# Block attention and gated MLP on one core: a first load on another queue, a transpose on another engine, and load issues at another place in the order

## Chip, cores and metric

One core of a Trainium2 chip runs the whole program. The metric is device time in microseconds of one execution; the lower, the better. The three executions shown of the kernel before took 164.96, 169.21 and 168.84 us, with a median of 168.84 us. The profiled execution is the one of 164.96 us.

## The reference, cut to what matters

There are 4 batches of 8 heads, 768 rows and 64 columns per head. A row of `q`, `k`, `v` blocks is 96 long, and there are 8 blocks.

```
P = sort_net                                  # (4, 8, 8, 8)
for _ in range(5):                            # Sinkhorn
    P = exp(P - max(P, -1));  P = P / sum(P, -1);  P = P / sum(P, -2)
k_sorted, v_sorted = P mixes the 8 blocks of k and of v
scores = q_block @ k_sorted_block.T / 8       # 96 x 96, block by block
x = softmax(scores) @ v_sorted_block          # -> (4, 768, 512)
h = relu(x @ w_in);  u, v = halves of h
v_s = w_spatial @ normalize(v) + b_spatial
out = (u * v_s) @ w_out                       # (4, 768, 512) float32
```

## The kernel before

**Inputs.** `load_heads` (L91) loads one batch of `q`, `k` or `v` as a tile of 128 partitions, 8 heads and 384 columns. The source is fp32 and the tile bf16; the DMA is issued by POOL and casts on the way. The tiles `q_in`, `k_in` and `v_in` have two buffers each, so batches 0 and 1 are loaded at the start. POOL's issues stand in this order: q and k of batch 0 (L101, L102), v of batch 0 (L128), `w_in` (L130), the bias (L131), `w_spatial` (L133), v, k and q of batch 1 (L134 to L136), `w_out` (L138). Among them POOL builds an identity and two selection masks (`ident_bf`, `a16`, `sel16`). SP carries the small load of `sort_net` (L88), the two-step turn of the mixed v through HBM (`vd`, `vb`, L263 and L264), and the results.

**The mixing matrix.** `sinkhorn` (L150) alternates one exponential on ACT (L152) with six small operations on DVE, five times, and leaves `p_bf` of 32 partitions (batch and head) by 8 by 8. `spread_t` (L177) turns it with eight matmuls and a DVE copy into `pt`; `spread` (L189) then spreads it over 128 partitions with one matmul and a DVE copy into `prep_sb`. `make_pdiag` (L199) multiplies that by a mask and gives `pdiag`, one 128 x 128 matrix per head, by which the matmuls of `ktr`, `vtr` and `vmix` mix blocks. Batch 0 is spread before the schedule. Its other three batches come by steps P and R in the schedule, with their `make_pdiag` on POOL.

**The order.** Inside `manual_schedule` the order of PE, DVE, ACT and POOL is written out by hand in `SCHEDULE` (L482). A step such as `k30A1` is a unit (`k`), its index (3), the batch (0), the engine that empties PSUM (A for ACT, D for DVE) and one of four PSUM buffers (1). Units of attention: `k` and `q` transpose, `v` (and `t`, `B` for batch 0) mixes v, `s` scores with an exponential on ACT, `a` attends and takes a logarithm on ACT, `d` divides. Units of the MLP: `V`, `N` (normalize), `U`, `S` (spatial matmul), `O` (output), `w` turns `w_spatial`. The MLP of one batch is interleaved with the attention of the next. Each engine takes its own instructions strictly in that order.

**The gates.** A unit S of the MLP (L437) adds the bias on DVE (`vs`, L454, two buffers) and multiplies by `u` on POOL (`gt`, L455); in the last batch DVE does both, in halves of 384 columns. Four `gt` feed the O units, in the order of their index. Before the first S of batches 0 and 1, POOL copies one element of each half of the next batch's `vb` (`gate`, L537). That makes it wait until both halves have landed. It then issues the loads of v, q and k for the batch after (L540 to L542), and only then its first `gt`.

**Elsewhere.** `warm` (L167) issues matmuls whose result nobody reads.

Of the kernel before, what the change touches and what calls it, by code (L numbers as in the profile page):

```python
# [8 lines left out]
FP32 = mybir.dt.float32  # L9
BF16 = mybir.dt.bfloat16  # L10
# [19 lines left out]
def kernel(  # L30
# [12 lines left out]
    nc = tc.nc  # L43
# [18 lines left out]
    pd_pool = ctx.enter_context(tc.tile_pool(name="pd", bufs=B))  # L62
    ld = ctx.enter_context(tc.tile_pool(name="ld", bufs=2))
    att = ctx.enter_context(tc.tile_pool(name="att", bufs=2))
    qk_pool = ctx.enter_context(tc.tile_pool(name="qk", bufs=7))
    ex_pool = ctx.enter_context(tc.tile_pool(name="ex", bufs=7))
# [3 lines left out]
    vs_pool = ctx.enter_context(tc.tile_pool(name="vs", bufs=2))  # L70
# [20 lines left out]
    def load_heads(x, b, name):  # L91
# [9 lines left out]
    q_in[0] = load_heads(q, 0, "q_in")  # L101
    k_in[0] = load_heads(k, 0, "k_in")  # L102
# [10 lines left out]
    sel16 = const.tile([8, 128], BF16)  # L113
    nc.gpsimd.memset(sel16, 0.0)
    nc.gpsimd.affine_select(
        out=sel16.rearrange("p (j t) -> p j t", t=TB),
        in_=sel16.rearrange("p (j t) -> p j t", t=TB),
        pattern=[[1, NB], [0, TB]], compare_op=ALU.not_equal,
# [54 lines left out]


    pts = {}

    def spread_t(b, nb, ps):  # L177
# [19 lines left out]
    pdiag = [pd_pool.tile([128, H, NB, TB], BF16, name="pdiag") for _ in range(B)]  # L197

    def make_pdiag(b, eng, h0, n):  # L199
        eng.tensor_mul(  # L200
            out=pdiag[b][:, h0:h0 + n],
            in0=_raw_ap(mask16, 0, [mask16.ap[0], [0, n], [TB, NB], [1, TB]]),
            in1=_raw_ap(prep_sb, b * NB * H + h0, [prep_sb.ap[0], [1, n], [H, NB], [0, TB]]),
        )
# [29 lines left out]
    class Attention:  # L234
# [147 lines left out]
    class Gmlp:  # L382
# [54 lines left out]
        def spatial(self, mc, eng, ps):  # L437
            t = ps_tile(ps)
            pairs = [(g, x) for g in range(G) for x in range(2)]
            if self.last:  # L440
                pairs = [(g, x) for x in range(2) for g in range(G)]
# [11 lines left out]
            for x in (slice(0, 1), slice(1, 2)) if self.last else (slice(0, 2),):  # L453
# [29 lines left out]
        k00A0 k30A1 k20D2 s00-3 k10D0 s70-1 s50-2 t30D3 t10A0 t00D1 s20-2 s60-3 B30D0 s10-1  # L483
        B10D2 s30-3 t20D0 a70-1 s40-2 B00D3 d70-- a20-0 B20D2 d20-- a00-3 a10-1 d00-- a40-2
        d10-- d40-- a30-0 a50-3 d30-- a60-1 P00-2 d50-- d60-- R00-0 V00-2 w50A3 w30A1 V10-0
        w40D2 v11A3 V20-1 v01A0 U00D3 v21A2 v31A1 U10A0 w20D2 w10D1 w00A3 k11D0 k21A2 q01D1
        k01A3 q11D0 k31D2 N00-- s31-1 U20A3 s11-0 s21-1 S00-2 s61-3 s41-0 U30A1 s51-2 s01-3
        S10-0 a01-1 d01-- a41-2 d41-- S20-3 a11-0 a51-1 d51-- d11-- S30-2 s71-3 a21-1 a61-0
        a31-2 d61-- d31-- O20A3 a71-0 d21-- O10A2 d71-- O00A3 V01-1 V21-2 v02A0 V11-3 v12A1
        U01A2 U11D0 N01-- v22A3 v32A1 U21A2 k12A0 q12D3 k02A1 q02A2 k22A0 k32A3 S01-1 s42-2  # L490
        s02-0 S11-3 s72-1 s52-2 S21-0 s32-3 s22-1 U31A2 a42-0 a02-3 d42-- d02-- s12-1 S31-2
        s62-0 a32-3 a72-1 d32-- a12-2 d72-- d12-- O21A0 a52-3 d52-- a22-1 a62-2 d22-- d62--
        O01D0 O11D3 V02-1 V22-2 v03A0 V12-3 v13A1 U02A2 U12D0 N02-- v23A3 v33A1 U22A2 k13A0
        q13D3 k03A1 q03A2 k23A0 k33A3 S02-1 s43-2 s03-0 S12-3 s73-1 s53-2 S22-0 s33-3 s23-1
# [82 lines left out]
```

The softmax here doesn't subtract the row's maximum and nothing guards it: scores larger than these inputs give would overflow.

## Time and profile before

| what | value |
| --- | --- |
| profiled execution, its own time | 164.96 us |
| its span (first to last instruction) | 163.2 us |
| three executions, median | 168.84 us (164.96 to 169.21) |
| PE busy | 147.4 us, 90% of the span |
| ACT, DVE, POOL busy | 109.9, 97.4, 42.8 us |
| landing of q, k, v of batch 0, from the span's start | 8.6, 12.4, 16.2 us |
| landing of v, k, q of batch 1 | 32.9, 36.8, 40.7 us |

The span is counted from the first recorded instruction to the last. The 1.76 us between the span and the execution's own time lie around it. A landing is an issue's start plus the time to landing that the profile gives for it. The chain of waits follows the work that ended last back from the end: at each step to what released it, or to the instruction before it on its engine. PE is busy 12.68 us of the 13 from 28 to 41 us, 49.74 of the 50 from 89 to 139 us, and 18.38 of the last 25.

### The profile page before, as it was taken

The numbers are of one execution on the slowest core, as the hardware profiler recorded it, in microseconds if no ns is written. First come the engines' busy times: TensorE is split into PE (matmuls) and PEld (weight loads), VectorE is DVE, ScalarE is ACT, GpSimd is POOL, SyncE is SP. The second block draws the span as 40 slices with busy tenths as digits, with TensorE's granted clock in tenths as the row PEclk, the third lists the DMA queues.
The fourth block names the chain that finished last, engine by engine and source line by source line (L and its number), as shares of the span: only waits on it lengthen the run. The fifth ranks groups of instructions, "written<-read, shape, count | busy, mean of one in ns | idle before, by whom it ended". The sixth has DMA issues, their size and how long they took to land.

```text
span 163.2 us, 3907 instructions
## 1 busy us (share of the span) xinstructions
PE 147.4 (90%) x1636; PEld 86.1 (53%) x1645; DVE 97.4 (60%) x203; ACT 109.9 (67%) x181; POOL 42.8 (26%) x46
## 2 busy tenths in 40 slices
PE   0969995999999999999995999999999999999770
PEld 0246872557756544457663544468556444565330
DVE  4667877468952652489222448785244478849951
ACT  3166999678787678689946892799778955550040
POOL 7941000890019740000069420000352400000000
PEclk9999999999999999999999999999999999999999
DMA  2999999999956999515429993525300036000055
GB/s 14 194 204 207 214 269 189 204 204 216 280 144 78 203 203 253 231 52 167 152 33 183 204 230 118 223 96 197 96 4 0 4 135 257 0 0 4 0 192 193
DMA packets 21554, 23.86 MB, mean 146 GB/s; under 512 B 736, under 2 KB 18144, under 8 KB 21408
## 3 DMA queue, kind: packets, MB, share of 16 engines
q0 software_dynamic: 13760, 12.58, 48.3%
q1 hardware_dynamic: 7776, 11.02, 18.8%
q8 instruction: 13, 0.21, 0.5%
q14 instruction: 5, 0.04, 0.1%
HBM read 27.14 MB, written 8.65 MB: 219 GB/s over the span
## 4 chain that ended last, share of the span: by engine, by line
PE 53%; DMA 24%; POOL 7%; DVE 6%; issue 6%; ACT 2%; DVEq 0%; POOLq 0%; SPq 0%
DMA q_in<-in_q_dram 19%; PE ps L443 13%; PE ps L465 10%; PE ps L393 9%; PE ps L428 8%; PE ps L352 4%; DVE vs L454 3%; PE ps L331 3%; PE ps L359 2%; DMA vb<-vd 2%; DVE gt L455 2%; PE ps L276 2%; POOL k_in L93 2%; DMA vd<-vm 1%; POOL v_in L93 1%
## 5 line engine op out<-in xcount | busy, mean ns | idle before, releaser
L443 PE MATMUL ps<-wspT,v_sb 128*128 128x384 bf16 x192 | 33.4, 327 | 0.0
L338 ACT ACTIVATE ex<-ps 96x768 bf16<-96x768 f32 x32 | 24.3, 806 | 7.0 <-PE ps L331 6.9
L454 DVE TENSOR_TENSOR vs<-ps,b_bc 128x768 f32<-128x768 f32 (+1 forms) x20 | 15.9, 795 | 21.6 <-PE ps L443 17.4
L375 DVE TENSOR_TENSOR xt<-ps,lns 128x384 bf16<-128x384 f32 x32 | 16.9, 554 | 19.7 <-ACT lns L371 19.7
L455 POOL TENSOR_TENSOR gt<-vs,u_sb 128x768 bf16<-128x768 f32 x12 | 19.6, 1653 | 31.5 <-ACT ex L338 29.7
L443 PEld LDWEIGHTS <-v_sb 128*128 128x128 bf16 x192 | 17.8, 98 | 11.8 <-issue 0.4
L465 PE MATMUL ps<-w_out_sb,gt 128*128 128x512 bf16 x90 | 21.9, 380 | 1.1 <-DVE gt L455 0.8
L428 PE MATMUL ps<-xt,w_in_sb 128*128 128x384 bf16 x128 | 22.6, 326 | 0.0
L393 PE MATMUL ps<-w_in_sb,xt 128*128 128x512 bf16 x94 | 22.1, 379 | 0.1
L407 DVE BATCH_NORM_STATS2 stats<-v_sb 128x6 f32<-128x512 bf16 x24 | 16.3, 678 | 8.5 <-ACT v_sb L227 8.4
L227 ACT ACTIVATE v_sb<-ps 128x1024 bf16<-128x1024 f32 (+1 forms) x15 | 12.5, 852 | 12.9 <-PE ps L393 12.9
L221 ACT COPY o_sb<-ps 128x256 f32<-128x256 f32 (+1 forms) x11 | 7.3, 663 | 13.8 <-DVE o_sb L223 12.1
L428 PEld LDWEIGHTS <-w_in_sb 128*128 128x128 bf16 x128 | 12.2, 98 | 8.1
L365 ACT ACTIVATE lns<-ps 128x384 f32<-128x384 f32 x32 | 14.4, 486 | 3.0 <-PE ps L359 3.0
L371 ACT ACTIVATE lns<-lns 128x384 f32<-128x384 f32 x32 | 15.7, 525 | 0.2
L465 PEld LDWEIGHTS <-gt 128*128 128x128 bf16 x96 | 8.6, 98 | 12.4 <-DVE gt L455 1.3
L393 PEld LDWEIGHTS <-xt 128*128 128x128 bf16 x96 | 9.2, 98 | 10.9 <-DVE xt L375 0.8
L352 PE MATMUL ps<-ex,vb 96*64 96x96 bf16 x256 | 11.3, 209 | 2.6 <-DVE vs L454 1.7
L352 PEld LDWEIGHTS <-vb 96*64 96x64 bf16 x256 | 8.6, 109 | 7.7 <-issue 6.4
L227 ACT ACTIVATE u_sb<-ps 128x768 bf16<-128x768 f32 x13 | 10.3, 808 | 1.7 <-PE ps L428 1.2
L221 ACT CAST kT<-ps 128x768 bf16<-128x768 f32 x13 | 10.0, 805 | 1.8 <-PE ps L288 1.8
L359 PE MATMUL ps<-ex,ones 96*64 96x384 bf16 x64 | 10.8, 326 | 0.0
(73 smaller groups left out, 174.5 us busy)
## 6 DMA issues: line engine op xcount, KB each, us to landing
out_dram<-o_sb SPq DMA_DIRECT2D x9, 512.0 KB, 2.8
q_in<-in_q_dram POOLq DMA_DIRECT2D x4, 768.0 KB, 10.3
k_in<-in_k_dram POOLq DMA_DIRECT2D x4, 768.0 KB, 13.6
v_in<-in_v_dram POOLq DMA_DIRECT2D x4, 768.0 KB, 9.7
vd<-vm SPq DMA_DIRECT2D x6, 384.0 KB, 4.0
vb<-vd SPq DMA_DIRECT2D x6, 384.0 KB, 3.7
out_dram<-o_sb SPq DMA_DIRECT2D x6, 256.0 KB, 2.1
wsp_nat<-in_moe_w_spatial_dram POOLq DMA_DIRECT2D x1, 1152.0 KB, 22.2
```

The lines of the kernel that those rows point to most:

```text
L221: nc.scalar.copy(out=out, in_=in_)
L227: nc.scalar.activation(out=out, in_=in_, func=AF.Relu)
L338: nc.scalar.activation(out=e.rearrange("p h i c -> p h (i c)"), in_=t[0:BLK, :, 0:NB // 2 * BLK], func=AF.Exp, scale=scale,)
L352: nc.tensor.matmul(t[hh * 64:hh * 64 + 64, 0, ii * BLK:(ii + 1) * BLK], lhsT=self.vb[:, i, h // (H // 2), h % (H // 2), :], rhs=self.e[n][ ...
L375: nc.vector.tensor_mul(out=self.xt[hp].rearrange("p (g i t) -> p i g t", g=G, i=NB)[:, i0:i0 + NB // 2], in0=t[:, 0, 0:HW].rearrange("p (i ...
L393: nc.tensor.matmul(t[:, x, :], lhsT=self.xt[kc][:, g * 128:(g + 1) * 128], rhs=w_in_sb[:, kc, DH:DFF], start=(kc == 0), stop=(kc == KC - 1),)
L407: nc.vector.bn_stats(out=stats, in_=v_sb[:, x, :])
L428: nc.tensor.matmul(t[:, x, 0:HW], lhsT=w_in_sb[:, kc, mc * 128:(mc + 1) * 128], rhs=self.xt[kc][:, x * HW:(x + 1) * HW], start=(kc == 0), ...
L443: nc.tensor.matmul(t[:, x, 0:HW], lhsT=self.v[g][:, mc * 128:(mc + 1) * 128], rhs=wspT[:, g, x * HW:(x + 1) * HW], start=(g == 0), stop=(g ...
L454: nc.vector.tensor_add(out=vs[:, x], in0=t[:, x, 0:HW], in1=b2[:, x])
L455: eng.tensor_mul(out=gt2[:, x], in0=vs[:, x], in1=u2[:, x])
L465: nc.tensor.matmul(t[:, x, :], lhsT=self.gt[mc][:, g * 128:(g + 1) * 128], rhs=w_out_sb[:, mc, :], start=(mc == 0), stop=(mc == FC - 1),)
```

## The change

The first q goes through SP's hardware queue as fp32 into a tile `q_first` and is cast by two copies on POOL and two on ACT. The ACT copies stand in the fourth round of Sinkhorn, and the transposes of q in the fifth. The tile `wsp_nat` takes over the buffer of `q_first`. The load of k stands behind the masks on POOL, and one mask is larger (32 x 512). `p_bf` is turned by two DVE transposes once for all batches; eight matmuls spread it. The first two heads of `pdiag` are made from PSUM. Batches 1 to 3 are spread at the schedule's start. In each attend of batch 0 three matmuls of 128 columns are added, whose result nobody reads. The gate and the loads behind it stand before the third S instead of the first. In the last batch only the last S stays on DVE in halves; the other three are whole, with `gt` on POOL. `ex` has eight buffers (seven before), `vs` three (two before). The schedule is written anew for batches 0 and 1; for 2 and 3 only PSUM buffers 0 and 2 change places.

```diff
--- before.py
+++ after.py
@@ -60,14 +60,15 @@
     const = ctx.enter_context(tc.tile_pool(name="const", bufs=1))
     pers = ctx.enter_context(tc.tile_pool(name="pers", bufs=1))
     pd_pool = ctx.enter_context(tc.tile_pool(name="pd", bufs=B))
+    stage = ctx.enter_context(tc.tile_pool(name="stage", bufs=1))
     ld = ctx.enter_context(tc.tile_pool(name="ld", bufs=2))
     att = ctx.enter_context(tc.tile_pool(name="att", bufs=2))
     qk_pool = ctx.enter_context(tc.tile_pool(name="qk", bufs=7))
-    ex_pool = ctx.enter_context(tc.tile_pool(name="ex", bufs=7))
+    ex_pool = ctx.enter_context(tc.tile_pool(name="ex", bufs=8))
     xt_pool = ctx.enter_context(tc.tile_pool(name="xt", bufs=8))
...
-    vs_pool = ctx.enter_context(tc.tile_pool(name="vs", bufs=2))
+    vs_pool = ctx.enter_context(tc.tile_pool(name="vs", bufs=3))
     vsb_pool = ctx.enter_context(tc.tile_pool(name="vsb", bufs=4))
     o_pool = ctx.enter_context(tc.tile_pool(name="osb", bufs=3))
     small = ctx.enter_context(tc.tile_pool(name="small", bufs=4))
@@ -98,8 +99,10 @@
 
     v_in, k_in, q_in = {}, {}, {}
 
-    q_in[0] = load_heads(q, 0, "q_in")
-    k_in[0] = load_heads(k, 0, "k_in")
+    q_first = stage.tile([128, H, G * D], FP32, name="q_first", tag="stage")
+    nc.sync.dma_start(
+        out=q_first, in_=_raw_ap(q, 0, [[G * D, 128], [S * D, H], [1, G * D]]),
+    )
     ident_bf = const.tile([128, 128], BF16)
     make_identity(nc, ident_bf)
     a16 = const.tile([16, 128], BF16)
@@ -110,12 +113,12 @@
         pattern=[[0, NB], [1, TB]], compare_op=ALU.not_equal,
         fill=1.0, base=0, channel_multiplier=-1,
     )
-    sel16 = const.tile([8, 128], BF16)
-    nc.gpsimd.memset(sel16, 0.0)
+    sel = const.tile([BH, NB // 2, 128], BF16)
+    nc.gpsimd.memset(sel, 0.0)
     nc.gpsimd.affine_select(
-        out=sel16.rearrange("p (j t) -> p j t", t=TB),
-        in_=sel16.rearrange("p (j t) -> p j t", t=TB),
-        pattern=[[1, NB], [0, TB]], compare_op=ALU.not_equal,
+        out=sel.rearrange("p i (j t) -> p i j t", t=TB),
+        in_=sel.rearrange("p i (j t) -> p i j t", t=TB),
+        pattern=[[NB, NB // 2], [1, NB], [0, TB]], compare_op=ALU.not_equal,
         fill=1.0, base=0, channel_multiplier=-1,
     )
     eps_tile = const.tile([128, 1], FP32)
@@ -125,11 +128,19 @@
     ones = const.tile([BLK, D], BF16)
     nc.vector.memset(ones, 1.0)
 
+    k_in[0] = load_heads(k, 0, "k_in")
     v_in[0] = load_heads(v, 0, "v_in")
+    q_in[0] = ld.tile([128, H, G * D], BF16, name="q_in", tag="q_in")
+    def cast_q(hp, copy_op):
+        x = slice(2 * hp, 2 * hp + 2)
+        copy_op(out=q_in[0][:, x, :], in_=q_first[:, x, :])
+    cast_q(0, nc.gpsimd.tensor_copy), cast_q(1, nc.gpsimd.tensor_copy)
     w_in_sb = pers.tile([128, KC, DFF], BF16)
     nc.gpsimd.dma_start(out=w_in_sb, in_=moe_w_in.rearrange("(kc p) f -> p kc f", p=128))
     nc.gpsimd.dma_start(out=b_nat, in_=_raw_ap(moe_b_spatial, 0, [[0, 128], [1, S]]))
-    wsp_nat = pers.tile([128, G, S], BF16)
+    wsp_nat = stage.tile([128, G, S], BF16, name="wsp_nat", tag="stage")
     nc.gpsimd.dma_start(out=wsp_nat, in_=moe_w_spatial.rearrange("(p g) s -> p g s", g=G))
     v_in[1] = load_heads(v, 1, "v_in")
     k_in[1] = load_heads(k, 1, "k_in")
@@ -147,9 +158,11 @@
     rowsum = small.tile([BH, NB], FP32, tag="sk")
     colsum = small.tile([BH, NB], FP32, tag="sk2")
 
-    def sinkhorn():
+    def sinkhorn(between):
         for n in range(5):
             nc.scalar.activation(out=p_all, in_=p_all, func=AF.Exp)
+            for step in between.get(n, ()):
+                step()
             nc.vector.reduce_sum(out=rowsum, in_=p_all, axis=AX.X)
             nc.vector.reciprocal(out=rowsum, in_=rowsum)
             nc.vector.tensor_mul(
@@ -171,36 +184,41 @@
 
     prep_sb = pers.tile([128, B, NB, H], BF16)
 
...
+    pdiag = [pd_pool.tile([128, H, NB, TB], BF16, name="pdiag") for _ in range(B)]
+    def make_pdiag(b, eng, h0, n, src=None):
+        base = h0 if src is not None else b * NB * H + h0
+        src = prep_sb if src is None else src
+        eng.tensor_mul(
+            out=pdiag[b][:, h0:h0 + n],
+            in0=_raw_ap(mask16, 0, [mask16.ap[0], [0, n], [TB, NB], [1, TB]]),
+            in1=_raw_ap(src, base, [src.ap[0], [1, n], [H, NB], [0, TB]]),
+        )
+    p_t = pers.tile([BH, 2, BH], BF16)
+    def transpose_p():
+        for x in range(2):
+            nc.vector.transpose(
+                out=p_t[:, x, :], in_=p_bf[:, x * (NB // 2):(x + 1) * (NB // 2), :].rearrange("p i j -> p (i j)"),
+            )
+    def spread(b, nb, ps):
         n = nb * NB * H
         t = ps_tile(ps)
         for i in range(NB):
             nc.tensor.matmul(
-                t[0:NB, 0, 0:n].rearrange("p (b i h) -> p b i h", i=NB, h=H)[:, :, i, :],
-                lhsT=p_bf[:, i, :], rhs=ident_bf[0:BH, b * H:(b + nb) * H],
+                t[:, 0, 0:n].rearrange("p (b i h) -> p b i h", i=NB, h=H)[:, :, i, :],
+                lhsT=sel[:, i % (NB // 2), :],
+                rhs=p_t[:, i // (NB // 2), b * H:(b + nb) * H],
                 start=True, stop=True,
             )
-        pts[b] = small.tile([NB, B * NB * H], BF16, name="pt", tag="pt", bufs=2)
-        nc.vector.tensor_copy(out=pts[b][:, 0:n], in_=t[0:NB, 0, 0:n])
-    def spread(b, nb, ps):
-        n = nb * NB * H
-        t = ps_tile(ps)
-        nc.tensor.matmul(t[:, 0, 0:n], lhsT=sel16, rhs=pts[b][:, 0:n], start=True, stop=True)
+        if b == 0:
+            make_pdiag(0, DVE, 0, 2, t.rearrange("p x c -> p (x c)"))
         nc.vector.tensor_copy(
             out=prep_sb[:, b:b + nb].rearrange("p b i h -> p (b i h)"), in_=t[:, 0, 0:n],
-        )
...
     b_bc = pers.tile([128, S], FP32)
@@ -346,6 +364,12 @@
         def attend(self, n, eng, ps):
             hp, ih = n // 2, n % 2
             t = ps_tile(ps)
+            if self.b == 0:
+                for _ in range(3):
+                    nc.tensor.matmul(
+                        t[:, 1, HW:512], lhsT=ident_bf, rhs=warm_sb[:, 0:512 - HW],
+                        start=True, stop=True,
+                    )
             for ii in range(NB // 2):
                 for hh in range(2):
                     h, i = 2 * hp + hh, ih * (NB // 2) + ii
@@ -437,7 +461,8 @@
         def spatial(self, mc, eng, ps):
             t = ps_tile(ps)
             pairs = [(g, x) for g in range(G) for x in range(2)]
-            if self.last:
+            final = self.last and len(self.gt) == FC - 1
+            if final:
                 pairs = [(g, x) for x in range(2) for g in range(G)]
             for g, x in pairs:
                 nc.tensor.matmul(
@@ -450,7 +475,7 @@
             gt2, u2, b2 = (
                 y.rearrange("p (x c) -> p x c", x=2) for y in (gt, self.u[mc], b_bc)
             )
-            for x in (slice(0, 1), slice(1, 2)) if self.last else (slice(0, 2),):
+            for x in (slice(0, 1), slice(1, 2)) if final else (slice(0, 2),):
                 nc.vector.tensor_add(out=vs[:, x], in0=t[:, x, 0:HW], in1=b2[:, x])
                 eng.tensor_mul(out=gt2[:, x], in0=vs[:, x], in1=u2[:, x])
             self.gt[mc] = gt
@@ -480,21 +505,21 @@
 
 
     SCHEDULE = """
...
+        R00-0 k00A1 k20D2 k30A3 k10D0 s00-1 s10-2 t00D3 s50-0 t10D1 s60-2 B00D3 s30-0 B10D1
+        s40-2 t20D3 s20-0 t30D1 a10-2 s70-3 B20D0 d10-- a00-1 d00-- a20-3 a40-0 B30D2 d20--
+        d40-- a30-1 d30-- a50-2 a60-3 d50-- a70-0 d60-- d70-- V00-1 w00D2 w20A3 V10-0 w30A1
+        V20-3 w10A2 U30A0 v01D1 v31A3 U10A2 k21D0 k01A3 q01D1 k31A2 k11A0 q11D3 s11-1 U20D2
+        v11A0 w40D3 N00-- U00D1 w50A2 v21A0 S20-3 s31-2 s41-0 S10-1 s21-3 s01-2 S00-0 s61-1
+        a01-3 a11-2 d11-- d01-- s51-0 S30-1 s71-2 a41-3 a31-0 d41-- a61-1 d31-- d61-- O00A2
+        a51-3 d51-- a21-0 a71-1 d71-- d21-- O10D2 O20A3 V01-1 V21-0 v02A2 V11-3 v12A1 U01A0
+        U11D2 N01-- v22A3 v32A1 U21A0 k12A2 q12D3 k02A1 q02A0 k22A2 k32A3 S01-1 s42-0 s02-2
+        S11-3 s72-1 s52-0 S21-2 s32-3 s22-1 U31A0 a42-2 a02-3 d42-- d02-- s12-1 S31-0 s62-2
+        a32-3 a72-1 d32-- a12-0 d72-- d12-- O21A2 a52-3 d52-- a22-1 a62-0 d22-- d62-- O01D2
...
     """
     UNITS = {
         "v": "vmix", "k": "ktr", "q": "qtr", "s": "score", "a": "attend", "d": "divide",
@@ -504,20 +529,21 @@
     with tc.manual_schedule(engines={ET.PE, ET.DVE, ET.Activation, ET.Pool}):
         attn = {b: Attention(b) for b in range(B)}
         gmlp = {}
-        sinkhorn()
         warm(9, 1)
-        attn[0].qtr(0, ACT, 2), attn[0].qtr(1, ACT, 3)
-        spread_t(0, 1, 0), warm(1, 1)
+        sinkhorn({
+            3: [lambda: cast_q(2, nc.scalar.copy), lambda: cast_q(3, nc.scalar.copy)],
+            4: [lambda: attn[0].qtr(0, ACT, 2), lambda: attn[0].qtr(1, ACT, 3)],
+        })
+        transpose_p()
+        warm(1, 1)
         spread(0, 1, 0)
-        make_pdiag(0, DVE, 0, 2), make_pdiag(0, DVE, 2, 6)
-        warm(4, 1)
+        make_pdiag(0, DVE, 2, 6)
+        warm(1, 1)
         for step in SCHEDULE.split():
             name, n, b = step[0], int(step[1]), int(step[2])
             eng = {"A": ACT, "D": DVE, "-": None}[step[3]]
             ps = None if step[4] == "-" else int(step[4])
-            if name == "P":
-                spread_t(1, 3, ps)
-            elif name == "R":
+            if name == "R":
                 spread(1, 3, ps)
                 for x in range(1, B):
                     make_pdiag(x, nc.gpsimd, 0, H)
@@ -531,7 +557,7 @@
                 if b not in gmlp:
                     gmlp[b] = Gmlp(b)
                 if name == "S":
-                    if not gmlp[b].gt and b + 2 < B:
+                    if len(gmlp[b].gt) == 2 and b + 2 < B:
                         gate = small.tile([1, 2], BF16, name="gate", tag="gate")
                         for x in range(2):
                             nc.gpsimd.tensor_copy(
@@ -540,7 +566,7 @@
                         v_in[b + 2] = load_heads(v, b + 2, "v_in")
                         q_in[b + 2] = load_heads(q, b + 2, "q_in")
                         k_in[b + 2] = load_heads(k, b + 2, "k_in")
-                    eng = DVE if b == B - 1 else nc.gpsimd
+                    eng = DVE if b == B - 1 and len(gmlp[b].gt) == FC - 1 else nc.gpsimd
                 getattr(gmlp[b], UNITS[name])(n, eng, ps)
             else:
                 getattr(attn[b], UNITS[name])(n, eng, ps)
```

More of the change, by code (lines that the diff above doesn't have):

```diff
@@ L172 @@
     prep_sb = pers.tile([128, B, NB, H], BF16)
-    pts = {}
-    def spread_t(b, nb, ps):
+    pdiag = [pd_pool.tile([128, H, NB, TB], BF16, name="pdiag") for _ in range(B)]
[14 more added lines that the diff above has]
+    def spread(b, nb, ps):
         n = nb * NB * H
@@ L181, in spread_t @@
             nc.tensor.matmul(
-                t[0:NB, 0, 0:n].rearrange("p (b i h) -> p b i h", i=NB, h=H)[:, :, i, :],
-                lhsT=p_bf[:, i, :], rhs=ident_bf[0:BH, b * H:(b + nb) * H],
+                t[:, 0, 0:n].rearrange("p (b i h) -> p b i h", i=NB, h=H)[:, :, i, :],
+                lhsT=sel[:, i % (NB // 2), :],
+                rhs=p_t[:, i // (NB // 2), b * H:(b + nb) * H],
                 start=True, stop=True,
             )
-        pts[b] = small.tile([NB, B * NB * H], BF16, name="pt", tag="pt", bufs=2)
-        nc.vector.tensor_copy(out=pts[b][:, 0:n], in_=t[0:NB, 0, 0:n])
-    def spread(b, nb, ps):
-        n = nb * NB * H
-        t = ps_tile(ps)
-        nc.tensor.matmul(t[:, 0, 0:n], lhsT=sel16, rhs=pts[b][:, 0:n], start=True, stop=True)
+        if b == 0:
+            make_pdiag(0, DVE, 0, 2, t.rearrange("p x c -> p (x c)"))
         nc.vector.tensor_copy(
             out=prep_sb[:, b:b + nb].rearrange("p b i h -> p (b i h)"), in_=t[:, 0, 0:n],
-        )
[L197 to L203, printed above, removed]
         )
@@ L482 @@
     SCHEDULE = """
[L483 to L494, printed above, removed]
@@ L495 @@
-        U32A2 a43-0 a03-3 d43-- d03-- s13-1 S32-2 s63-0 a33-3 a73-1 d33-- a13-2 d73-- d13--
-        O22A0 a53-3 d53-- a23-1 a63-2 d23-- d63-- O02D0 O12D3 V03-1 V13-2 V23-0 N03-- U03A3
-        U13A1 U23A2 U33A0 S03-3 S13-1 S23-2 S33-0 O03A3 O13A1 O23A2
+        R00-0 k00A1 k20D2 k30A3 k10D0 s00-1 s10-2 t00D3 s50-0 t10D1 s60-2 B00D3 s30-0 B10D1
+        s40-2 t20D3 s20-0 t30D1 a10-2 s70-3 B20D0 d10-- a00-1 d00-- a20-3 a40-0 B30D2 d20--
+        d40-- a30-1 d30-- a50-2 a60-3 d50-- a70-0 d60-- d70-- V00-1 w00D2 w20A3 V10-0 w30A1
@@ new lines @@
+        a32-3 a72-1 d32-- a12-0 d72-- d12-- O21A2 a52-3 d52-- a22-1 a62-0 d22-- d62-- O01D2
+        O11D3 V02-1 V22-0 v03A2 V12-3 v13A1 U02A0 U12D2 N02-- v23A3 v33A1 U22A0 k13A2 q13D3
+        k03A1 q03A0 k23A2 k33A3 S02-1 s43-0 s03-2 S12-3 s73-1 s53-0 S22-2 s33-3 s23-1 U32A0
+        a43-2 a03-3 d43-- d03-- s13-1 S32-0 s63-2 a33-3 a73-1 d33-- a13-0 d73-- d13-- O22A2
+        a53-3 d53-- a23-1 a63-0 d23-- d63-- O02D2 O12D3 V03-1 V13-0 V23-2 N03-- U03A3 U13A1
+        U23A0 U33A2 S03-3 S13-1 S23-0 S33-2 O03A3 O13A1 O23A0
```

## The prediction, made before the changed kernel ran

> **What bounds the kernel now.** I read the table of stretches first, then the chain of waits, then the timelines of the places that the change touches. Columns of the stretches: length, then busy time and instruction count of PE, PEld, DVE, ACT, POOL, then clock, DMA share and GB/s.
>
> ```profile
> 13.00:28.00 15.00, 12.87 (x283) 9.59 (x281) 11.75 (x19) 14.21 (x27) 0.43 (x1) 1.00 1.13 222
> 28.00:41.00 13.00, 12.68 (x118) 7.78 (x120) 8.96 (x20) 9.52 (x13) 7.45 (x4) 1.00 1.30 208
> 65.00:89.00 24.00, 22.27 (x253) 13.57 (x253) 11.78 (x24) 18.29 (x24) 6.06 (x7) 1.00 0.52 138
> 139.00:164.00 25.00, 18.38 (x104) 9.92 (x103) 15.12 (x34) 6.74 (x14) 0.00 (x0) 0.97 0.17 64
> ```
>
> From 13 to 28 us ACT is full (14.21 of 15). From 28 on PE is, except for one hole before 89 and the tail. The chain of waits (start, length, what):
>
> ```profile
> 9.08 31.58 DMA q_in<-in_q_dram
> 40.66 0.04 issue
> ...
> 85.09 0.90 POOL k_in L93
> 85.99 1.68 POOL gt L455
> 87.67 0.02 issue
> 87.69 0.97 DVE vs L454
> 88.66 0.04 issue
> 88.71 0.36 PE ps L352 x8
> ```
>
> The load of q for batch 1 lands at 40.66 us, just when PE wants it: DMA and PE are tied there. The hole at 87 is a chain gate, three load issues, `gt`, `vs`, and then an attend. The timelines of POOL and, for the tail, of all engines price it:
>
> ```profile
> 82.77 0.18 POOL L537 COPY gate<-vb 1x1 bf16<-1x1 bf16 x1 [4.33 <-DMA vb<-vd]
> 83.29 0.94 POOL L93 DMA_DIRECT2D v_in<-in_v_dram  x1 [0.35 <-PE ps L331]
> 84.23 0.89 POOL L93 DMA_DIRECT2D q_in<-in_q_dram  x1
> 85.09 0.90 POOL L93 DMA_DIRECT2D k_in<-in_k_dram  x1
> 85.98 4.86 POOL L455 TENSOR_TENSOR gt<-vs,u_sb 128x768 bf16<-128x768 f32 x3
> ```
>
> ```profile
> 154.19 4.06 PE L465 MATMUL ps<-w_out_sb,gt 128*128 128x512 bf16 x18 [0.81 <-DVE gt L455]
> ```
>
> From the second gate to the first `gt` it is 85.98 - 82.77 = 3.2 us, and by the timeline PE then sat 1.68 us. In the tail PE sat 0.81 us for the last `gt`.
>
> [...]v of batch 0 and what follows land one after the other (3.8 us from q to k). [...]PE's longest gap after its first work is 1.68 us here[...]. The changed start leaves PE idle from about 8.2 to 10.
>
> **The change part by part.** All against the profiled execution: span 163.2 us, own time 164.96.
>
> *First load.* SP issues it after `sort_net`, at 0.74 + 0.38 = 1.12 us. Results of 256 KB land in 2.1 us and of 512 KB in 2.8, so 256 KB cost 0.7 us on a base of 1.4; 1536 KB make 1.4 + 6 x 0.7 = 5.6 us. It lands at 6.7 instead of 8.6. Ends: 6.4 (no base) to 8.5 (as slow as q took before, 7.3). POOL builds its masks first. They took 1.1 us; the larger one adds perhaps 1 us; so k is issued at about 3.1, behind q in the engines. k, v, `w_in`, bias, `w_spatial`, v, k, q took 40.7 - 8.6 = 32.1 us one after the other. So q of batch 1 lands at 6.7 + 32.1 = 38.8 instead of 40.7: -1.9 us, I take -1.8. This needs POOL's issues to stay ahead of the engines. Behind the two casts on POOL stand all seven later loads. A cast of 768 columns costs [...]1.56 (copy of `b_bc`); I take 1.2. POOL is free at 9.1, `w_in` is issued by 9.9, and v, two loads of 3.8 after 6.7, ends at 14.3: covered by over 2 us even at 1.56. `w_spatial` waits for ACT's casts too (9.6): also covered.
>
> *Casts on ACT* stand before the fifth exponential. 8.0 + 2 x 0.8 = 9.6 against 9.48 before: +0.1 on the Sinkhorn chain. If q landed after 7.95, each us would cost one. The copies of qT then run 10.0 to about 13.0 instead of 9.65 to 12.4; the first kT is wanted at 13.2, the first scores at 15.2. Covered.
>
> *The turn of P.* Before, from `p_bf` (11.2): mask 0.27, matmuls 0.34, `pt` 0.21, matmul 0.18, `prep_sb` 0.22, `pdiag` 0.42 + 0.95, to 13.87. After: mask, two transposes ([...]I take the 0.21 of `pt`), matmuls 0.34, two heads 0.42, `prep_sb` 0.22, six heads 0.95: to 13.85. Only the first k comes 0.5 earlier. What ACT does next waits for the six heads, so this gains about nothing. The early spread of batches 1 to 3 puts 0.35 (`prep_sb`) before a kT on DVE, and takes P and R (a wait of 1.0, 0.6 of matmuls, 0.33 of DVE) out at 26.5 to 28.1. POOL's three `pdiag` (5.9 us) move to about 15 to 21, where POOL is idle.
>
> *Batch 0.* ACT loses one kT (0.80), and starts its scores 0.15 later. Walking its queue with these durations, I get the last division 0.3 us earlier. The 24 small matmuls at 56 ns[...] are 1.3 us, in the 2.1 us that PE is idle in this stretch; without cover 0.17 per attend. Then PE has V 3 x 1.73, four w at 0.39, U 2 x 1.4, two v and two k at 0.33, about 10 us from 28.5: it wants q of batch 1 at 38.6. So DMA still ends that wait, and the gain there is its 1.8.
>
> *Moved behind q.* Two w and two v units now come after it: 2 x 0.39 + 2 x 0.33 = +1.4 us, since PE is full there.
>
> *First gate.* Let t0 be the end of PE's last v unit of batch 1. In batch 2 its counterpart was 73.8, and `vb` let the gate go at 82.8: 9.0 us. Four S (2.06 each), seven scores and five attends take 12.1, so O starts at t0 + 12.1. POOL passes the gate at 9.0, spends 3.2 on issues, and only then does the third `gt` (1.64): t0 + 13.85. That third one is index 0, which O needs first. PE waits 1.7 us; the last `gt` ends at 15.5 and costs 0.35 as before. Before, S began only after the gate was nearly open and nothing waited. So +1.7. Ends: 0 (`vd` and `vb` undisturbed, 6.1 instead of 7.6) to 3.6 (`vd` at the 5.8 of batch 1).
>
> *Second gate.* It stands behind two `gt` and opens at 82.8 anyway. The issues end at 88.6, the third `gt` at 90.3, before O; a third `vs` buffer frees DVE. The wait of 1.68 goes: -1.7. The later loads have time: v lands at 93, wanted at 103.5.
>
> *Tail.* Three `gt` of 1.64 on POOL, one per S of 2.06, keep pace; the third ends at 152.9. DVE has only the last S in halves: its first `gt` ends at 153.3 instead of 154.1, and PE's 0.81 goes: -0.8 (0 if POOL lags).
>
> Sum: -1.8 + 1.4 + 1.7 - 1.7 - 0.8 = -1.2. Span 162.0, own time 163.8. The median shown is 3.9 above the profiled time; -1.2 on it gives **167.6**.
>
> **Rivals.** *Forecast (0.50)*: the stall moves from the second gate to the first. *No new stall (0.25)*: `vb` lands 1.5 us sooner; for it speaks that half 0 has a head start, against it that in batch 2 it had the same. Then -1.2 - 1.7 = -2.9: 165.9. *PE wants more than DMA gives (0.12)*: q on the hardware queue writes fp32, and takes the engines as long as it saves; q of batch 1 lands at 40.7. Then -1.2 + 1.8: +0.6, 169.4. *Slower (0.13)*: the ACT casts hold Sinkhorn. They stand before the fifth exponential, and DVE's last six operations, the spread and all of batch 0 wait behind. If q lands at L, it costs L - 7.95; no longer faster from L = 9.2, and over 2% slower from 12.5. At L = 10.5 it is +1.4: 170.2. With `vb` at its slow end too, +3.3.[...]
>
> **Numbers.** A measurement of this kernel can tell about 2% (3.3 us) from no change. Over 2% faster needs no new stall and another us, say from batch 0: 0.18. Slower: 0.13. Same: 0.69. The three runs differ by 4 us among themselves. A median from near the lowest would be about 163.8, and with no new stall 162; the range is 161.8 to 170.2. If the median stays where it was, the forecast's own range is 165.9 to 169.5.
>
> **What would show it.** q lands at 6.7 and at 38.8; PE's first wait behind the scores of batch 1 is an O for `gt`, about 1.7 us; none at `vs` in batch 1; no 0.8 in the tail. Wrong if exponential five starts after 9.7, if PE waits over 1 us for q, or if the first PE matmuls of batch 0 run at half pace.

## The result and the profile after

The changed kernel takes 167.87 us (median of 22 runs), the kernel before 166.56 (27 runs on the same chip). The ratio is 1.0095, 95% interval 1.0064 to 1.0126: about 1.6 us slower, where the prediction had -1.2. The ratio compares fast runs alone, which is why it is not the quotient of the two medians. The profiled execution took 167.19 us, its span is 165.4, so +2.2 against the span of before. Both profiled executions are among the quick ones of their kernel (fourth of 22, second of 27), and the working below is about these 2.2 us. The forecast of 167.6 stands close to the median by luck: its -1.2 was added to the 168.84 of the three runs first shown.

The stretches of the kernel after, cut as in the prediction (length, then busy time and count of PE, PEld, DVE, ACT, POOL, then clock, DMA share, GB/s):

```profile
13.00:28.00 15.00, 14.23 (x301) 10.68 (x302) 12.46 (x19) 13.26 (x22) 10.01 (x7) 1.00 1.13 224
28.00:41.00 13.00, 11.59 (x114) 6.86 (x115) 8.14 (x19) 9.43 (x14) 0.00 (x0) 1.00 1.26 199
65.00:89.00 24.00, 23.95 (x261) 14.14 (x257) 13.39 (x26) 19.44 (x28) 2.14 (x2) 1.00 0.75 188
```

ACT is no longer full from 13 to 28 us (13.26 of 15), PE has holes from 28 to 41 (11.59 of 13), and the hole before 89 is gone (23.95 of 24). The chain of waits after, its start and the first gate:

```profile
1.19 7.42 DMA q_first<-in_q_dram
8.66 1.60 POOL q_in L137 x2
10.31 2.13 PE ps L294 x36
...
54.73 1.98 issue
...
57.22 0.96 POOL v_in L94
58.19 0.89 POOL q_in L94
59.07 0.87 POOL k_in L94
59.94 1.68 POOL gt L480
...
62.50 2.37 PE ps L490 x6
```

The chain starts with the first q, which landed at 8.6 us, not 6.7. No load of batch 1 is on it: PE, not DMA, now sets when q of batch 1 is transposed. Then comes the first gate, as forecast: issues, then the third `gt`. The timelines show what PE paid there. First PE at this place before, where nothing waits, then POOL and PE after:

```profile
58.86 1.94 PE L465 MATMUL ps<-w_out_sb,gt 128*128 128x512 bf16 x7
```

```profile
56.73 0.18 POOL L563 COPY gate<-vb 1x1 bf16<-1x1 bf16 x1 [2.00 <-DMA vb<-vd]
```

```profile
61.67 0.61 PE L490 MATMUL ps<-w_out_sb,gt 128*128 128x512 bf16 x1 [2.17 <-POOL gt L480]
62.50 2.37 PE L490 MATMUL ps<-w_out_sb,gt 128*128 128x512 bf16 x6 [0.22 <-issue]
...
91.73 0.36 PE L376 MATMUL ps<-ex,vb 96*64 96x96 bf16 x8
...
154.94 5.61 PE L490 MATMUL ps<-w_out_sb,gt 128*128 128x512 bf16 x23
```

PE waits 2.17 us for the third `gt`, and its eight matmuls then take 3.2 us (61.67 to 64.87), where eight in a row take 1.8 to 2.0 elsewhere. The last two lines are the attend behind the second gate, without its 1.68 us of waiting, and the tail, without a wait for the last `gt`. Finer stretches of the kernel after show a granted clock of 0.72 at the start and of 0.93 around the first O unit; before it was 1.00 in each of these three:

```profile
8.00:14.00 6.00, 4.07 (x61) 2.91 (x61) 3.79 (x18) 4.50 (x5) 5.34 (x8) 0.72 1.32 205
14.00:32.00 18.00, 16.15 (x312) 11.49 (x314) 13.46 (x20) 14.38 (x26) 9.01 (x6) 1.00 1.16 221
47.00:70.00 23.00, 20.53 (x212) 11.28 (x212) 11.02 (x19) 14.87 (x27) 9.55 (x9) 0.93 0.82 155
```

Starts of the same work in both timelines (us from the span's start):

| work | before | after | difference |
| --- | --- | --- | --- |
| `p_bf` ready | 11.21 | 11.82 | +0.6 |
| first k matmul, batch 0 | 13.19 | 14.22 | +1.0 |
| first w (all V of batch 0 done) | 29.95 | 31.99 | +2.0 |
| first q transpose, batch 1 | 40.70 | 40.82 | +0.1 |
| first S, batch 0 | 45.04 | 47.17 | +2.1 |
| first V, batch 1 | 64.65 | 69.42 | +4.8 |
| first V, batch 2 | 100.06 | 103.09 | +3.0 |
| first V, batch 3 | 133.74 | 136.76 | +3.0 |
| end | 163.2 | 165.4 | +2.2 |

So the second gate and the tail give back 1.7 and 0.8, as forecast, but 4.8 are lost before 70 us.

### The profile page after: what moved, and what is told of

Its sections match the earlier page's. It is cut to its first block, busy times and chain, and to the rows that moved or that the text cites. A ratio compares the mean times of both kernels' runs of the same rounds, so it can differ in the third digit from the quotient of the medians.

```text
span 165.4 us, 3944 instructions
## 1 busy us (share of the span) xinstructions
PE 150.2 (91%) x1656; PEld 88.2 (53%) x1664; DVE 96.6 (58%) x196; ACT 109.9 (66%) x181; POOL 49.2 (30%) x50
## 4 chain that ended last, share of the span: by engine, by line
PE 77%; DMA 6%; POOL 5%; DVE 5%; issue 3%; ACT 2%; SPq 0%; DVEq 0%; POOLq 0%
PE ps L468 17%; PE ps L452 13%; PE ps L417 12%; PE ps L490 10%; DMA q_first<-in_q_dram 4%; PE ps L349 4%; PE ps L306 4%; PE ps L376 4%; PE ps L294 4%; PE ps L383 2%; PE ps L264 2%; POOL gt L480 2%; PE ps L333 1%; DVE vs L479 1%; PE ps L230 1%
## 5 line engine op out<-in xcount | busy, mean ns | idle before, releaser
L480 POOL TENSOR_TENSOR gt<-vs,u_sb 128x768 bf16<-128x768 f32 x15 | 24.7, 1649 | 99.0 <-DVE vs L479 70.4
L490 PE MATMUL ps<-w_out_sb,gt 128*128 128x512 bf16 x89 | 22.9, 395 | 2.8 <-POOL gt L480 2.2
L239 ACT COPY o_sb<-ps 128x256 f32<-128x256 f32 (+1 forms) x10 | 6.3, 628 | 16.5 <-DVE o_sb L241 11.3
L452 PEld LDWEIGHTS <-w_in_sb 128*128 128x128 bf16 x128 | 12.2, 98 | 7.9
L417 PEld LDWEIGHTS <-xt 128*128 128x128 bf16 x96 | 9.1, 98 | 12.2 <-DVE xt L399 2.0
L294 PE MATMUL ps<-ident_bf,q_in 128*64 128x128 bf16 x192 | 7.9, 240 | 3.8 <-POOL q_in L137 3.7
L349 PE MATMUL ps<-qT,kT 64*96 64x96 bf16 x256 | 10.5, 211 | 0.1
```

Of the source, the lines that this page charges most:

```text
L239: nc.scalar.copy(out=out, in_=in_)
L349: nc.tensor.matmul(t[0:BLK, hh, ii * BLK:(ii + 1) * BLK], lhsT=self.k[hp][rows, i * BLK:(i + 1) * BLK], rhs=self.q[hp][rows, i], start=Tru ...
L417: nc.tensor.matmul(t[:, x, :], lhsT=self.xt[kc][:, g * 128:(g + 1) * 128], rhs=w_in_sb[:, kc, DH:DFF], start=(kc == 0), stop=(kc == KC - 1),)
L452: nc.tensor.matmul(t[:, x, 0:HW], lhsT=w_in_sb[:, kc, mc * 128:(mc + 1) * 128], rhs=self.xt[kc][:, x * HW:(x + 1) * HW], start=(kc == 0), ...
L480: eng.tensor_mul(out=gt2[:, x], in0=vs[:, x], in1=u2[:, x])
L490: nc.tensor.matmul(t[:, x, :], lhsT=self.gt[mc][:, g * 128:(g + 1) * 128], rhs=w_out_sb[:, mc, :], start=(mc == 0), stop=(mc == FC - 1),)
```

## Experiments

Each ratio is to runs of the kernel before on the same chip, with its 95% interval. The edits are to the changed kernel unless it says "before".

**The first gate: loads behind the fourth `gt`** (`a_gate4`), or behind the third (`g_third_gt`). The edit shown is the second; the first moves the same block, for batch 0, behind the fourth S.

```diff
-                    if len(gmlp[b].gt) == 2 and b + 2 < B:
+                    if len(gmlp[b].gt) == (3 if b == 0 else 2) and b + 2 < B:
```

> The changed kernel, with the loads of batch 2 issued behind the fourth gt of batch 0 instead of the second. Theory (POOL's three load issues hold up the third gt, PE waits, and the wait of over 2 us halves PE's clock for the next 3 us): PE's wait at the first O unit (2.2 us) falls under 0.5 us, the granted clock of that stretch goes from 0.93 to 1.00, the eight matmuls of that O unit take about 1.8 us instead of 3.2, and the first V unit of batch 1 starts about 3.1 us after fewer: 66.5 instead of 69.6 us. The time falls by about 3 us, 1.9% below the changed kernel and about 1% below the kernel before. Rival 1 (the low clock in that stretch is a throttle that comes with the load, not with the wait): only the 2.2 us go. Rival 2 (the loads are now too late): PE waits for v of batch 2 at the first v unit after that, and what is gained is given back.

> The changed kernel with the loads of batch 2 issued behind the third gt of batch 0 (second in the changed kernel, fourth in the run in which k of batch 2 came too late). Theory (POOL's issues held up the gt that the first O unit reads first): that gt is now done at about 58, before PE wants it; only the last gt (index 3) stands behind the issues and is done at 61.6, against 60.6 when PE wants it. PE's wait falls from 2.2 to about 1.0 us, the clock stays at 1.00 between 47 and 70, the first V unit of batch 1 starts at about 66.8 instead of 69.4, and the loads start no later than before, so that nothing waits for k of batch 2. Time 2.5 us below the changed kernel, about 0.6% below the kernel before. Rival (k of batch 2 is at its limit already): PE waits for k of batch 2 at about 76 and the gain is lost.

Behind the fourth: 1.0366 (1.0312 to 1.0419). The wait before the first O is gone, the clock is 1.00 from 47 to 70, V of batch 1 starts at 66.6, 18.83 us after the first S (22.25 in the change):

```profile
60.03 1.90 PE L490 MATMUL ps<-w_out_sb,gt 128*128 128x512 bf16 x8
```

But the loads are late. From the list of waits of PE:

```profile
PE ps L306 <- DMA k_in<-in_k_dram: 4.4, 1, 4.4
PE ps L294 <- POOL q_in L137: 3.3, 1, 3.3
PE ps L183 <- POOL ident_bf masks.py:199: 1.5, 1, 1.5
PE ps L264 <- DMA v_in<-in_v_dram: 1.3, 1, 1.3
```

In batch 2 PE waits 4.4 us for k and 1.3 for v; k took 19.7 us from issue to landing, and the clock fell to 0.90 from 70 to 103. The gate is thus no mere obstacle: moved too far, it costs more than it held up. Behind the third: 0.9977 (0.9947 to 1.0006), against 1.0095 of the change. The wait moves to the last `gt` and is 1.09 us, the clock is 1.00 from 47 to 70, S to V of batch 1 takes 19.97 us instead of 22.25, and no load is waited for:

```profile
63.66 0.60 PE L490 MATMUL ps<-w_out_sb,gt 128*128 128x512 bf16 x2 [1.09 <-POOL gt L480]
```

V itself started at 68.81 and not at the 66.8 expected: in this execution PE ran at half pace up to about 18 us, and S came 1.7 us later than in the change.

**Only the idle time filled** (`k_filled_wait`): `warm(8)` ahead of the first O of batch 0; nothing that O waits for is changed.

> The changed kernel with eight matmuls of 512 columns, whose result nobody reads, just ahead of the first O unit, where PE waits 2.2 us. They take 1.7 us of that wait. Theory (it is the idle time that halves the clock): the O unit still starts at about 61.7, but its eight matmuls take 1.8 us instead of 3.2, the clock between 47 and 70 is 1.00 instead of 0.93, and the first V unit of batch 1 starts 1.4 us sooner (68.0). Rival (the clock is lowered for the load of the chip, by more work and not by less): the clock stays at 0.93 or falls further, and V starts no sooner.

1.0034 (1.0004 to 1.0064). The stretch and the O unit of this kernel:

```profile
47.00:70.00 23.00, 22.19 (x229) 11.99 (x227) 11.66 (x20) 15.28 (x27) 9.56 (x9) 1.00 0.80 156
```

```profile
62.27 2.20 PE L490 MATMUL ps<-w_out_sb,gt 128*128 128x512 bf16 x8 [0.66 <-POOL gt L480]
```

With the same gate, but PE busy, the clock stays at 1.00 and the eight matmuls take 2.2 us instead of 3.2. So about 1 us of the loss at the gate is half clock after the wait, not the wait. S to V takes 21.57 us, 0.7 less than in the change, where 1.4 were expected (V at 69.02, not 68.0).

**v units ahead of q** (`q2_v_ahead`): the cause of the late `vb`. The lines of the schedule are joined into one.

```diff
-U10A2 k21D0 k01A3 q01D1 k31A2 k11A0 q11D3 s11-1 U20D2 v11A0 w40D3 N00-- U00D1 w50A2 v21A0 S20-3
+U10A2 v11D1 v21A0 k21D3 k01A1 q01D2 k31A3 k11A0 q11D1 s11-3 U20D2 w40D0 N00-- U00D1 w50A2 S20-3
```

> The changed kernel, with the last two v units of batch 1 (v1, v2) moved ahead of k2 and q0 of batch 1, as far ahead as in the kernel before. Theory (the first gate is late because the change moved these v units behind q, so the turned v starts later): vb lands about 3 us earlier, the wait before the first O falls from 2.2 us to under 0.6, the clock stays 1.00 from 47 to 70 us, first V of batch 1 at about 66.9 instead of 69.4, ratio to before about 0.995. Rival (the turn through HBM is slow by itself[...]): vb comes as late, the wait stays at 2 us and the ratio at 1.01.

0.9967 (0.9942 to 0.9992), V of batch 1 at 66.33. POOL and PE there, and the stretch:

```profile
54.88 0.30 POOL L563 COPY gate<-vb 1x1 bf16<-1x1 bf16 x2
```

```profile
59.76 2.02 PE L490 MATMUL ps<-w_out_sb,gt 128*128 128x512 bf16 x8
```

```profile
47.00:70.00 23.00, 22.98 (x234) 12.31 (x233) 12.65 (x22) 15.86 (x28) 9.46 (x9) 1.00 0.85 147
```

Neither POOL nor PE waits: `vd` and `vb` are issued from 41.4 and 45.7 instead of 45.9 and 49.0. S to V of batch 1 takes 18.84 us, 3.4 less than in the change, with the loads where the change put them. The theory holds and the rival falls: with these two v units ahead of q the first gate doesn't stall. With the gate behind the fourth `gt` it doesn't either (18.83 us in `a_gate4`), so the stall takes both, the late v units and the gate ahead of the third `gt`.

**The start: PE kept busy until q lands** (`d_long_warm`): `warm(25, 1)` for `warm(9, 1)`.

> The changed kernel with 25 instead of 9 matmuls ahead of the first transposes, so that PE works until about 9.3 us instead of 5.8. Theory (the 3.7 us without work halve PE's clock; the 48 transposes of q take 2.9 us instead of 1.66 and hold the spread of P, which is ready at 12.2, until 12.9): the transposes take about 1.7 us, the clock between 8 and 14 us is 1.0 instead of 0.72, the first k comes at about 13.5 instead of 14.2 us. At the end at most 0.7 us. Rival (the first k is late because of Sinkhorn alone): the transposes are faster, and the first k comes at 14.0 or later.

0.9911 (0.9876 to 0.9945). The clock is 1.00 from 8 to 14 us, and the 48 transposes take 1.7 us instead of 2.9:

```profile
9.88 0.53 PE L294 MATMUL ps<-ident_bf,q_in 128*64 128x128 bf16 x12 [0.73 <-POOL q_in L137]
10.65 1.20 PE L294 MATMUL ps<-ident_bf,q_in 128*64 128x128 bf16 x36 [0.25 <-POOL q_in L137]
```

The first k comes 0.5 us earlier although q landed later (7.8 us after its issue), S 0.46 earlier, and at the gate the second half of `vd` landed after 2.9 us instead of 4.4, so that the O wait was 0.91 and no half clock followed it:

```profile
59.94 2.20 PE L490 MATMUL ps<-w_out_sb,gt 128*128 128x512 bf16 x8 [0.91 <-POOL gt L480]
```

S to V takes 19.98 us, so most of the gain of this profile is at the gate and not in the 0.5 us of the start. The two may belong together. Among the profiles with the v units behind q, the second half of `vd` took 2.8 to 3.1 us where it was issued by 48.3 (here, in `b_no_fill` and in `h2_gate3_warm`), and 4.4 to 4.7 in the six where it was issued at 48.6 or later, the change among them. Why the later ones are slower no run shows.

**The first load undone** (`j_q_by_pool`): q of batch 0 by `load_heads` again, first on POOL, no casts; all else as changed.

> The changed kernel with its first part undone: the first q is loaded by POOL with the cast, as before, no casts on ACT and POOL, and w_spatial has its own buffer. All else as in the changed kernel. Theory (the first part delays batch 0 and brings the loads of batch 1 forward only 1 us, which nobody uses): P is ready at 11.2 instead of 11.8, the transposes of q start at 8.6 with 2.8 us without work before them and so at half pace, the first k comes at about 13.0 instead of 14.2, and V of batch 0 ends about 1 us sooner; q of batch 1 lands at 40.7 instead of 39.7 and PE waits for it up to 0.7 us. So the S units of batch 0 start at about 46.9 against 47.2, and the time is within 0.5 us of the changed kernel, but for the wait at the first O unit, which can be 1 to 2.4 us in either. Rival (the first part gains): 1 us slower than the changed kernel.

1.0084 (1.0053 to 1.0114), the same as the change within these intervals. `p_bf` is ready at 11.61, the first k at 13.43, q of batch 1 is transposed at 41.12. V of batch 0 didn't end 1 us sooner: the first w comes at 32.29 against 31.99. PE had waited 1.67 us for a mask at 12.2, and 36 matmuls of the first k took 1.92 us instead of 1.20. Taken together, no gain and no loss of the hardware queue shows at the end.

**k issued later** (`e_k_later`): a memset of the k tile ahead of its load.

> The changed kernel with a memset of the whole k tile on POOL ahead of its load, so that the load of k is issued about 2.6 us later (4.7 instead of 2.1 us). The memset changes no result. Theory (k on the software queue shares the DMA engines with the first q from about 4 us on, which is why q landed at 8.6 and not at 6.7): q lands at about 7.0, the fifth exponential starts at 9.5 instead of 10.1, and P is ready at 11.2 instead of 11.8. k lands at about 12 as before. Rival (a load of 1536 KB takes 7.4 us on the hardware queue by itself): q still lands at about 8.6, and k later than before.

1.0177 (1.0114 to 1.024), and inconclusive: k was issued at 5.5 and q landed after 6.5 us, but in `b_no_fill`, with k where the change has it, after 6.7, and over the profiles with the changed start it varies from 6.7 to 7.8. `p_bf` came at 12.21, and this line of DVE shows part of why:

```profile
4.86 0.76 DVE L170 TENSOR_TENSOR p_all<-p_all,rowsum 32x64 f32<-32x64 f32 x1
```

This product of two tiles takes 0.21 us elsewhere. Here it ended at 5.62, just after POOL's operation on a mask (4.75 to 5.59), which the memset had pushed there; another one, beside POOL's first cast of q, took 0.76 too. Beside the memset itself, from 2.1 to 4.8 us, the operations of DVE took their usual 0.19 to 0.26. The change has the same effect at a small size (0.36 instead of 0.21 beside the casts).

**No fill matmuls in batch 0** (`b_no_fill`): the 24 small ones in `attend` left out.

> The changed kernel without the 24 matmuls of 128 columns in the attends of batch 0. Theory (they stand on PE's chain at 0.27 us per attend, and batch 0 was late by more than the start alone): the first V unit ends 1 to 2 us sooner than 32.0 us, but q of batch 1 lands at 39.7 and is wanted at 41.0, so at most 1.3 us of it reach the end; time 0.3 to 1.3 us lower. Rival (they keep the clock up in batch 0): without them the granted clock falls below 1.0 between 20 and 32 us and V ends no sooner.

0.9968 (0.9937 to 0.9999). Its last V matmuls, and those of the change:

```profile
28.99 2.31 PE L411 MATMUL ps<-w_in_sb,xt 128*128 128x512 bf16 x5 [0.86 <-DVE xt L393]
```

```profile
30.90 1.25 PE L417 MATMUL ps<-w_in_sb,xt 128*128 128x512 bf16 x5 [0.87 <-DVE xt L399]
```

From the first k to this point it takes 28.99 - 13.21 = 15.78 us without and 30.90 - 14.22 = 16.68 with the fill, so the fill costs 0.9. But without it the five matmuls run at half pace, 2.31 us instead of 1.25, which takes that back (clock 0.91 from 14 to 32), so theory and rival are each right in part. The better ratio comes from elsewhere, in this profile from two places: the O wait was 1.29 us with no half clock behind it, and the first k came 1.0 us earlier than in the change, though the start is the same, because q landed at 7.9 and not at 8.6.

**The terms that held, alone on the kernel before**: the tail part (`f_last_gates_only`), and with it the second gate (`m2_before_two`; batch 0's gate, start and schedule as before).

```diff
...
-                    if not gmlp[b].gt and b + 2 < B:
+                    if len(gmlp[b].gt) == (0 if b == 0 else 2) and b + 2 < B:
...
-                    eng = DVE if b == B - 1 else nc.gpsimd
+                    eng = DVE if b == B - 1 and len(gmlp[b].gt) == FC - 1 else nc.gpsimd
```

The edit also has the third `vs` buffer and, as in the change, the halves for the last S alone.

> The kernel before with one part of the change: in the last batch the first three S units are whole with gt on POOL, and only the last stays on DVE in halves. Theory (this part does what it says): PE's wait of 0.81 us for the last gt goes and the end comes 0.8 us sooner, 0.5% below the kernel before. Rival (POOL lags behind DVE): no change or slower.

> The kernel before, with only the two parts of the change that did what was forecast: in batch 1 the loads stand behind the second gt (third vs buffer with it), and in the last batch three gt go to POOL. Batch 0's gate stays in front of its first S; start and schedule are untouched. If the terms of the prediction's sum add up, the second-gate wait (1.68 us) and the tail wait (0.8) go and nothing else moves: span 163.2 - 2.5 = 160.7, ratio to before 0.985. If the later loads of batch 3 collide with results on the DMA engines, a wait of 1 us or more for v, k or q of batch 3 shows and the ratio is 0.99 or above.

0.9937 (0.9898 to 0.9977) for the tail, 0.9861 (0.9783 to 0.994) for both: 163.5 us against 165.65, that is -2.3 of the -2.5 that the two terms add up to. In its profile neither wait is left; the attend behind the second gate and the tail:

```profile
88.02 0.36 PE L352 MATMUL ps<-ex,vb 96*64 96x96 bf16 x8
...
151.23 5.61 PE L466 MATMUL ps<-w_out_sb,gt 128*128 128x512 bf16 x24
```

It beats both kernels and has the lowest ratio measured, from four runs and with a wide interval.

**Repairs joined** (`h2_gate3_warm`: long warm and third `gt`; `r2_combo`: long warm and v ahead).

> The changed kernel with two edits that were each measured alone: 25 warm matmuls at the start, and the loads of batch 2 behind the third gt instead of the second. If the two remove different losses, half clock at the start and the wait before the first O, the gains add: clock 0.99 or more in all stretches, wait before the first O about 1.0 us, V of batch 1 at about 65.5 to 66.5, span 162, ratio to before 0.985 to 0.99. If the later loads take back what the gate gives, as they did behind the fourth gt, PE waits for k of batch 2 and the ratio stays at 0.99 or above.

> The changed kernel with 25 warm matmuls at the start and with v1 and v2 of batch 1 ahead of k2 and q0. If the late start of the turned v is the cause of the first gate's wait, this removes both the half clock at the start and the wait, without moving the loads: V of batch 1 at about 65.5, clock 0.99 or more everywhere, span about 161.5, ratio 0.98 to 0.985. If the turn is slow by itself, it stays at what the warm matmuls gave alone: ratio 0.99.

0.9903 (0.987 to 0.9935) and 0.9891 (0.9833 to 0.9949). In both the clock is 1.00 up to 103 us and V of batch 1 starts at 66.59 and 66.05, later than hoped: batch 0 still takes 17.8 us from first k to first w against 16.76 before. They can't be told from `d_long_warm` alone, nor, at these intervals, from `m2_before_two`. That the gains would add fully was wrong: `d_long_warm` already had a short O wait.

## Why the prediction was wrong, step by step

| step | forecast | measured | from |
| --- | --- | --- | --- |
| q of batch 1 | -1.8 | +0.1 | its first transpose, 40.70 to 40.82 |
| moved units | +1.4 | +1.2 | +2.0 from there to S, -0.8 from S to V in `q2_v_ahead` (18.84) against before (19.61) |
| first gate | +1.7 | +3.4 | S to V of batch 1, 22.25 against 18.84 in `q2_v_ahead` |
| second gate | -1.7 | -1.7 | V of batch 1 to V of batch 2, 35.41 to 33.67 |
| tail | -0.8 | -0.8 | V of batch 3 to the end, 29.46 to 28.64 |
| sum | -1.2 | +2.2 | |

**The step that failed** is "So DMA still ends that wait, and the gain there is its 1.8". It fell twice. The load gave 1.0 and not 1.8: q of batch 1 landed at 39.7, since the first q took 7.4 us and not 5.6 and landed at 8.6, just past the upper end of 8.5; what follows it took 31.1 instead of 32.1. And PE was not there to use it. "I get the last division 0.3 us earlier" should have been 2.0 later: PE reached q at 40.82, over 1 us after it had landed. Two terms make that up, 1.0 by the first k, which the text had 0.5 earlier, and 1.0 from there to the first w.

The first is the start. Sinkhorn was held by ACT's casts: by the text's own L - 7.95 a landing at 8.61 costs 0.66, and `p_bf` came 0.61 later. This was the mechanism of the rival called Slower, at a small size. `b_no_fill`, with the same start and q at 7.9, agrees: its first k came at 13.21. Then PE idled 3.7 us and ran the transposes at half pace; before, then after:

```profile
8.59 1.66 PE L276 MATMUL ps<-ident_bf,q_in 128*64 128x128 bf16 x48 [0.34 <-DMA q_in<-in_q_dram]
```

```profile
9.53 2.91 PE L294 MATMUL ps<-ident_bf,q_in 128*64 128x128 bf16 x48 [3.72 <-POOL q_in L137]
```

The prediction named this gap as "from about 8.2 to 10" and gave it no price. It was from 5.8 to 9.5: the matmuls of `warm` wait for the identity, which POOL now builds before any load, and so they began at 1.46 instead of 3.90. `d_long_warm` gives a price: with the clock kept, the first k is 0.5 us earlier. The second is "1.3 us, in the 2.1 us that PE is idle". The trace of before supports its 56 ns for a matmul of 128 columns: twelve of them begin at 29.95, and what follows at 30.62.

```profile
29.95 0.83 PE L212 MATMUL ps<-ident_bf,wsp_nat 128*128 128x128 bf16 x12
30.62 1.89 PE L393 MATMUL ps<-w_in_sb,xt 128*128 128x512 bf16 x8
```

In the change the three of an attend take 0.26 to 0.28 us up to its own first matmul, where 0.17 was taken, and 0.9 us of the fill was on the path (`b_no_fill`), for an attend waits for them and the logarithm on ACT waits for the attend. Busy time that fits into the idle time of a stretch is hidden only if it stands in the holes; these stood ahead of the work that ACT waited for.

**The first gate** was right in mechanism. By the text, from the end of PE's last v unit (47.33), O is wanted after 12.1 us, the gate opens after 9.0 and the third `gt` ends after 13.85. It was 12.2, 9.4 and 14.3, and the wait 2.17 instead of 1.7. What was missing is the half clock behind a wait of that length, 3.2 us for eight matmuls instead of 1.8. It was also taken as the price of the gate's place alone. `q2_v_ahead` shows that without the moved v units it is nothing, and the text priced these only at their own PE time. The size is that of one execution: with the v units behind q, S to V took 22.25, 22.73 (`j_q_by_pool`) and 22.66 (`e_k_later`), but 19.98 and 20.36 where `vd` was quick (`d_long_warm`, `b_no_fill`), so the gate cost 1.1 to 3.9 us.

**Right**: second gate, tail and moved units, within 0.2 us. POOL's casts (0.82 us each; the 1.2 taken was the author's estimate) and the transposes of P (0.15, 0.21 taken) were covered as stated.

**Open** is why q on the hardware queue lands after 6.7 to 7.8 us (the text had k issued at about 3.1, and it was issued at 2.1, but `e_k_later` doesn't settle whether that matters), and why the second half of `vd` takes about 2.9 us in some executions and 4.4 or more in others. Of the 1.0 us between first k and first w, 0.9 is the fill; the rest is within what the order of batch 0 may cost. The new order of batches 0 and 1, the earlier spread of batches 1 to 3 and the eighth buffer of `ex` were not undone on their own.

## What to carry to other kernels

Moving a producer behind other work costs its own time and, far more, the lateness of what hangs on it: here two v units of 0.33 us each cost 3.4 us, in the profiled execution, at a gate 10 us later. Price a PE wait with the pace of what follows it: here waits of 0.9 to 1.3 us at an O unit cost little more than themselves, those of 2.2 to 2.5 up to 1.6 more, and one of 1.7 us did either. A load that lands sooner gains only if the engine that wants it arrives sooner too, so the walk of that engine must be forecast as carefully as the transfer.

## What the runs showed of the hardware

After a wait of 2.17 us in the change, 2.30 in `j_q_by_pool` and 2.54 in `e_k_later` the eight matmuls of the O unit took 3.2 to 3.5 us, while after 1.29 in `b_no_fill` they took 2.2. Near 1.7 us it went both ways. `f_last_gates_only` issues the same instructions as the kernel before up to the last batch. At the second gate PE waits 1.68 us in the one and 1.67 in the other, and the twelve S matmuls behind it take 2.12 and 3.64 us. The kernel before, then `f_last_gates_only`:

```profile
89.80 2.12 PE L443 MATMUL ps<-wspT,v_sb 128*128 128x384 bf16 x12
```

```profile
89.75 0.36 PE L352 MATMUL ps<-ex,vb 96*64 96x96 bf16 x8 [1.67 <-DVE vs L455]
...
90.96 3.64 PE L444 MATMUL ps<-wspT,v_sb 128*128 128x384 bf16 x12
```

Slow matmuls also came behind several holes close together. In `j_q_by_pool` a hole of 1.67 us that ended at 12.2 and two shorter ones, of 0.33 and 0.18 us, were followed by the 36 matmuls of k in 1.92 us; in the change, with holes of 0.33 and 0.18 there, they took 1.20. The kernel before and `m2_before_two` issue the same instructions up to 40 us; PE is busy 0.95 and 0.93 of the 2 us from 26 to 28, and yet the stretch from 30 to 32 us has clock 1.00 in the one and 0.50 in the other. Before, then `m2_before_two`, the V matmuls there:

```profile
28.04 2.07 PE L393 MATMUL ps<-w_in_sb,xt 128*128 128x512 bf16 x7
```

```profile
28.06 3.03 PE L393 MATMUL ps<-w_in_sb,xt 128*128 128x512 bf16 x8
```

The first V of batch 1 then starts at 65.70 in `m2_before_two` and at 64.65 before, which makes 1.05 us between two executions of the same instructions. Why the clock fell in the one and not in the other no run here shows.

The column of the granted clock does not show every such stretch. In `a_gate4` and `e_k_later` it reads 1.00 from 8 to 14 us, and the 48 transposes of q take 2.91 and 2.90 us all the same. The durations decide.
